# Nyström attention with a mixture of experts: expert index from averaged context rows, 32x32 blocks in the pseudo-inverse, another order

## The chip, the cores and the metric

The kernel runs on one core of one Trainium2 chip. Its metric is the device time of one execution in microseconds; the time before is the median of three runs, 215.47 us (214.98 to 217.77).

The core has five engines with a queue each: TensorE (PE in the rows; PEld is its weight load), VectorE (DVE), ScalarE (ACT), GpSimd (POOL) and SyncE (SP, which here issues nearly all transfers). An engine takes its instructions strictly in the order in which the program lists them, and waits on semaphores for the others.

## The reference

Inputs are q, k, v of shape 4 x 8 x 576 x 64 (batch, heads, rows, head size; q and k times 8), a gate 512 x 8, and for each of 8 experts a 512 x 1024 and a 1024 x 512 matrix. All is float32.

```python
q_lm, k_lm = mean of q, k over groups of 18 rows        # 32 landmarks a head
A = softmax(q @ k_lm.T / 8)    # 576 x 32
Bm = softmax(q_lm @ k_lm.T / 8)  # 32 x 32
C = softmax(q_lm @ k.T / 8)    # 32 x 576
Z = Bm.T / (norm1(Bm) * norminf(Bm) + 1e-6)
for _ in range(6): Z = 2 * Z - Z @ Bm @ Z
x = A @ Z @ C @ v              # per head; heads side by side: 2304 x 512

logits = x @ w_gate; e = argmax(logits, axis=1)
# a row keeps its expert only while that expert has had fewer than 576 rows
out = softmax weight of e * relu(x @ w1[e]) @ w2[e]     # 0 for rows not kept
```

The capacity of an expert, 576 rows, is the size of one batch. In the drawn inputs all 576 rows of a batch choose one expert: 0, 3, 6 and 0 for batches 0 to 3, so the rows of batch 3 find their expert full and are zero.

## The kernel before

The program handles four batches. For each it has a chain of attention work, and for batches 0 to 2 one expert (key 0 to 2) over the 576 rows; the output rows of batch 3 are written as zeros. A check at the end reads how many (batch, expert) pairs are still to do and, if there are any, runs a second pass for them (lines 930 to 943).

Attention of a batch: `landmarks` sums q and k over 18 rows (`lmq`, `lmk`; DVE or POOL). `scores` makes `psC` and `psA`; `cpath` takes the softmax of `psC`, transposes it (`ctp`, `CT`) and multiplies with v (`cvp`, then `CV`: 4 heads x 32 landmark rows of context, 64 wide, for each half `g` of the heads). `apath` takes the softmax of `psA` into `AW` and transposes it to `AT`. `chain` makes the 32x32 matrices `bp` of the eight heads, their softmax and norms (`bst`, `BB`, `cc`), and the pseudo-inverse, four heads at a time on 128 partitions. For batches 1 to 3 a round is one matmul a half (`pp`, line 320) of a 128x128 block-diagonal matrix (`PQ`, `PQn`), which DVE builds anew after each round: line 454 spreads five copies of a 32-column result against the mask `bmask`, 128x320, and line 455 adds W. Batch 0 keeps whole 128x128 blocks (ScalarE copies them) and has a second matmul `wp` a round. Six rounds end in `Wd`; with `CV` it gives `mtp` and `MT`, the 512 x 32 factor of x.

`route` makes the logits (`gp`, `Gg`, `ltp`, `lg`), the argmax (`ls`, `eq`, `idx`, `oh`), ranks of rows within an expert by matmuls with triangles (`rp`), the experts with rows still kept (`act`), and the first of them (`sel`, `fx`, `ei`, lines 647 to 655). `ei` is the index: SyncE loads it into a register (line 773) and only then issues the loads of `w1t` (line 736) and `w2t` (line 709).

The expert `ffn`: `gps` = w1 times MT (a row of x is A times a 32-row factor, so W1 is first contracted to 32 rows a head), split by ScalarE and DVE into `gh` and `gl`; `hps` = these times `ah`/`al` (the split AT), three matmuls for each product; relu and split (`rr`, `hx`); `yps` = `hx` times the split w2 (`wh`, `wl`), again three; scaled by `fac` and written.

What sets the order: every piece of work is a generator of steps with an engine, a planned cost and dependencies; `weave` (line 81) runs through all of them and emits the instructions in the order in which its own clock would start them. `CFG` holds numbers and letters found for it: priorities (`pr`, `fp`, `wl`, ...) and which engine does what (`lm`, `aw`, `rx`, `lo`). `wps` (line 914) are filler matmuls on zeros, emitted while PE has nothing before the first `yps`.

Of the kernel before, what the change touches and what calls it, by code (L numbers as in the profile page):

```python
# [9 lines left out]
F32 = mybir.dt.float32  # L10
# [4 lines left out]
ALU = mybir.AluOpType  # L15
# [65 lines left out]
def weave(streams, banks, fill=None):  # L81
# [6 lines left out]
    fast = False  # L88

# [19 lines left out]
    while ready:  # L109
        cand = {}  # L110
        first = None
        for s in ready:
            step = s[2]
            t = max(s[4], clk[step.eng])
            if step.res:
                r = res[step.res]
                i = nxt[step.res]
                late = [r[(i + x) % len(r)] for x in range(step.nres)]
                if None in late:
                    continue  # L120
                t = max(t, *late)
# [15 lines left out]
        end = clk[eng] = t + step.cost * (2 if eng == "P" and t < 6500 else 1)  # L137
        t = end + HOP[eng]
# [20 lines left out]
def nystrom_moe(ctx: ExitStack, tc: tile.TileContext, q, k, v, vtail, wgate, w1, w2, out, cap):  # L159
# [55 lines left out]
    nc.gpsimd.memset(wg, 0.0)  # L215
    SP = 128 * NT
# [51 lines left out]

    lmt = {}
# [4 lines left out]
    def landmarks(b):  # L274
        for g in range(NG):
            for nm in "qk":
# [14 lines left out]
                else:  # L291
                    yield Step("G", 1380, deps=ld, order=order, prev=False)
# [4 lines left out]
                    yield Step("G", 700)  # L297
                    nc.gpsimd.tensor_tensor(tr[:, :, 0:4], tr[:, :, 0:4], tr[:, :, 4:8], ALU.add)
                    yield Step("G", 430)
                    nc.gpsimd.tensor_tensor(tr[:, :, 0:2], tr[:, :, 0:2], tr[:, :, 2:4], ALU.add)  # L300
                    yield Step("G", 380)
                    nc.gpsimd.tensor_tensor(tr[:, :, 0:1], tr[:, :, 0:1], tr[:, :, 8:9], ALU.add)
                    yield Step("G", 380, name=f"lm{b}{g}{nm}")
# [7 lines left out]
    n4 = [128, NG, 4, 32]  # L311
    gr = [128, NG, 32]

    def spread(t, src, n, e="V"):
        (nc.vector if e == "V" else nc.gpsimd).tensor_tensor(t, src.unsqueeze(2).to_broadcast([128, NG, n, 32]),
                                bmask[:, 0:n, :].unsqueeze(1).to_broadcast([128, NG, n, 32]), ALU.mult)

    def bdmm(dst, t, rhs):
        for g in range(NG):
            nc.tensor.matmul(dst[:, g], lhsT=t[:, g, 0:4].rearrange("p h m -> p (h m)"), rhs=rhs[g],  # L320
                             start=True, stop=True)

    def V(c, **kw):
        return Step("V", c, **kw)

    def chain(b):
        p = Step("P", 267, deps=LM(b, 0) + LM(b, 1), order=([f"wd{b - 1}"] if b else []) + ([f"mt{b - 2}"] if b > 1 else []), name=f"bp{b}", res="ch",
# [16 lines left out]
        yield Step("A", 150)  # L344
# [3 lines left out]
        yield V(70)  # L348
# [3 lines left out]
        yield V(140)  # L352
        nc.vector.tensor_tensor(Bst, Bst, bst[:, 1, :].unsqueeze(2).to_broadcast(gr), ALU.mult)
        yield V(140)
        nc.vector.transpose(BT, Bst)
        rc = sm.tile([128, 2, NG], F32, tag="rc", name="rc")
        cc = sm.tile([128, 2, NG], F32, tag="cc", name="cc")

        def norms():
            yield V(200)  # L360
            nc.vector.tensor_reduce(out=rc, in_=BB, axis=AX.X, op=ALU.add)
            yield V(135)
            rcb = sm.tile([128, 2 * NG, 32], F32, tag="rcb", name="rcb", bufs=1)
            nc.vector.tensor_copy(rcb, rc.rearrange("p a g -> p (a g)").unsqueeze(2).to_broadcast([128, 2 * NG, 32]))
            yield V(200)
            rct = sm.tile([128, 2 * NG, 32], F32, tag="rct", name="rct", bufs=1)
            nc.vector.transpose(rct, rcb)
            yield V(200)
            nrm = sm.tile([128, 2, NG], F32, tag="nrm", name="nrm")
            nc.vector.tensor_reduce(out=nrm.rearrange("p a g -> p (a g)"), in_=rct, axis=AX.X, op=ALU.max)  # L370
            yield V(70)
            nc.vector.tensor_tensor(cc[:, 0, :], nrm[:, 0, :], nrm[:, 1, :], ALU.mult)
            yield V(70)
# [5 lines left out]
        full = CFG["sx"][b] == "F"  # L379
        e = CFG["s3"][3 * b]  # L380
        yield Step(e, 330 if e == "V" else 690)
        BTd = sm.tile(n4, F32, tag="bd", name="BTd", bufs=1)
        spread(BTd, BT, 4, e)
        p = Step("P", 434 if full else 350, res="ch", keep=True)
        yield p
        nb = 4 if full else 1
        bbp = pch.tile([128, NG, nb, 32], F32, tag="ch", name="bbp")
        bdmm(bbp.rearrange("p g a m -> p g (a m)"), BTd,
             [(BTd[:, g].rearrange("p h m -> p (h m)") if full else BT[:, g, :]) for g in range(NG)])
        yield V(527 if full else 330, free=p, deps=[f"cc{b}"])  # L390
# [588 lines left out]
```

## Time and profile before

| | before |
|---|---|
| median of 3 runs | 215.47 us (214.98 to 217.77) |
| span of the profiled execution, first to last instruction | 214.7 us |
| PE / PEld busy | 90% / 68% |
| DVE / ACT / POOL busy | 65% / 38% / 41% |
| moved | 31.88 MB, 149 GB/s on the mean |
| granted TensorE clock, mean | 0.973 |

The profiled execution's own time is its span, 214.7 us; the runs have some tenths around it. Matmuls overlap one another, so the busy time of PE is a union, and the price of one group in a dense stretch is read from the chain of waits, where pieces don't overlap. DVE too starts an instruction before the last has ended; the distance from start to start is its price there.

### The profile page before, as it was taken

Reading aid. Unit: us, or ns where it says so; the run is one execution under the profiler, and the core shown is the slowest. Engines: PE = TensorE matmul, PEld = TensorE weight load, DVE = VectorE, ACT = ScalarE, POOL = GpSimd, SP = SyncE. Lnnn points to the kernel's source line nnn. Section 1 sums busy time; section 2 is a strip of 40 time slices with the busy share of each in tenths; the row PEclk is TensorE's granted clock in tenths of the full one; section 3 lists DMA queues with packets and bytes.
Section 4 is the critical chain, followed back from the end, with each engine's and each line's share of the span. In section 5 each row is a group of like instructions: output and inputs, shape, how many; then the busy total and the mean of one; then the engine's idle time right before and its main releaser. Section 6 shows DMA issues by size and latency. Waiting matters only on the chain.

```text
span 214.7 us, 4895 instructions
## 1 busy us (share of the span) xinstructions
PE 194.1 (90%) x1822; PEld 145.6 (68%) x1826; DVE 138.7 (65%) x408; ACT 82.0 (38%) x209; POOL 88.8 (41%) x129
## 2 busy tenths in 40 slices
PE   7888998749997989999997989999999999999990
PEld 2345864235886766787866668978876889788880
DVE  3899989995889899998866547732017488221110
ACT  2052541214877555813024465760106667300000
POOL 8027998960499993010221993340000634300000
PEclk9999999675999999999999999999999999999998
DMA  6999938246899500101198620681117500011121
GB/s 196 362 341 373 360 137 260 78 157 234 298 358 328 187 0 3 24 3 49 50 322 256 206 102 0 197 293 27 49 52 221 172 3 0 6 27 49 49 78 34
DMA packets 17905, 31.88 MB, mean 149 GB/s; under 512 B 1520, under 2 KB 9616, under 8 KB 17872
## 3 DMA queue, kind: packets, MB, share of 16 engines
q1 hardware_dynamic: 17808, 31.46, 43.7%
q8 instruction: 16, 0.26, 0.5%
q14 instruction: 17, 0.14, 0.2%
q0 software_dynamic: 64, 0.02, 0.1%
HBM read 26.76 MB, written 4.72 MB: 147 GB/s over the span
## 4 chain that ended last, share of the span: by engine, by line
PE 64%; DVE 21%; DMA 6%; issue 2%; POOL 2%; ACT 1%; SPq 1%; ACTq 0%
PE yps L861 29%; PE hps L803 14%; DMA w2t<-in_w 4%; PE yps L866 4%; PE pp L320 4%; PE gps L577 3%; DMA kt<-in_k 2%; PE psA L466 2%; PE psC L466 2%; DVE lmk L289 2%; DVE sel L650 2%; PE cvp L517 1%; DVE AW L534 1%; PE ctp L500 1%; POOL wl L725 1%
## 5 line engine op out<-in xcount | busy, mean ns | idle before, releaser
L861 PE MATMUL yps<-wh,hx 128*128 128x512 f32 (+1 forms) x208 | 63.5, 379 | 0.0
L861 PEld LDWEIGHTS yps<-wh,hx 128*128 128x128 f32 x208 | 38.1, 188 | 7.1 <-issue 0.3
L861 PE MATMUL yps<-wl,hx 128*128 128x512 f32 (+1 forms) x104 | 38.8, 373 | 0.0
L725 POOL TENSOR_TENSOR wl<-w2t,wh 128x512 fp32r<-128x512 f32 x14 | 18.3, 1325 | 41.2 <-ACT wh L719 39.4
L826 POOL TENSOR_TENSOR hx<-rr,hx 128x288 fp32r<-128x288 f32 (+2 forms) x38 | 24.7, 668 | 14.8 <-ACT hx L817 14.5
L803 PE MATMUL hps<-ah,gh 128*128 128x288 f32 x96 | 29.5, 307 | 0.1
L878 DVE TENSOR_SCALAR yo<-yps,fac 128x512 f32<-128x512 f32 (+1 forms) x11 | 7.7, 701 | 32.6 <-PE yps L861 32.6
L803 PE MATMUL hps<-ah,gl 128*128 128x288 f32 x96 | 28.3, 295 | 0.0
L803 PE MATMUL hps<-al,gh 128*128 128x288 f32 x96 | 28.3, 295 | 0.0
L861 PEld LDWEIGHTS yps<-wl,hx 128*128 128x128 f32 x104 | 19.6, 189 | 3.2
L803 PEld LDWEIGHTS hps<-ah,gh 128*128 128x128 f32 x96 | 18.0, 188 | 1.8 <-ACT hx L820 0.4
L719 ACT CAST wh<-w2t 128x512 fp32r<-128x512 f32 x24 | 14.9, 620 | 8.6 <-DMA w2t<-in_w 7.2
L803 PEld LDWEIGHTS hps<-al,gh 128*128 128x128 f32 x96 | 18.0, 188 | 0.1
L803 PEld LDWEIGHTS hps<-ah,gl 128*128 128x128 f32 x96 | 18.0, 188 | 0.0
L320 PEld LDWEIGHTS pp<-PQn 128*128 128x128 f32 x76 | 10.2, 190 | 7.4 <-PE gps L577 3.8
L725 DVE TENSOR_TENSOR wl<-w2t,wh 128x512 fp32r<-128x512 f32 x10 | 9.4, 940 | 8.9 <-ACT wh L719 8.6
L815 ACT ACTIVATE rr<-hps 128x288 f32<-128x288 f32 x27 | 11.1, 413 | 9.7 <-PE hps L803 8.0
L320 PE MATMUL pp<-PQn 128*128 128x64 f32 (+2 forms) x76 | 11.8, 278 | 2.9 <-DVE PQn L455 1.1
L557 POOL TENSOR_TENSOR AW<-AW,amx 128x576 f32<-128x576 f32 x6 | 6.9, 1158 | 14.7 <-DVE amx L545 14.7
L914 PE MATMUL wps<-wt 128*128 128x512 bf16 x30 | 11.4, 526 | 1.3 <-DVE bef L234 1.3
L817 ACT CAST hx<-rr 128x288 fp32r<-128x288 f32 x27 | 11.7, 434 | 0.6
L828 DVE SCALAR_TENSOR_TENSOR hx<-hps,hx 128x224 fp32r<-128x224 f32 (+2 forms) x34 | 10.1, 333 | 2.8 <-ACT hx L820 2.6
(177 smaller groups left out, 355.6 us busy)
## 6 DMA issues: line engine op xcount, KB each, us to landing
w1t<-in_w SPq DMA_DIRECT2D x12, 512.0 KB, 4.9
w2t<-in_w SPq DMA_DIRECT2D x24, 256.0 KB, 4.3
vm<-in_v SPq DMA_DIRECT2D x8, 512.0 KB, 7.3
qt<-in_q SPq DMA_DIRECT2D x6, 576.0 KB, 7.8
kt<-in_k SPq DMA_DIRECT2D x6, 576.0 KB, 7.8
out<-yo SPq DMA_DIRECT2D x11, 256.0 KB, 2.1
qt<-in_q SPq DMA_DIRECT2D x4, 288.0 KB, 4.2
kt<-in_k SPq DMA_DIRECT2D x4, 288.0 KB, 5.4
```

What stands on the lines that cost most here:

```text
L320: nc.tensor.matmul(dst[:, g], lhsT=t[:, g, 0:4].rearrange("p h m -> p (h m)"), rhs=rhs[g], start=True, stop=True)
L466: nc.tensor.matmul(ps[a][32 * h:32 * h + 32, :HS], lhsT=lmt[b, g, stat][x, y], rhs=st[b][mov][g][x, y, HS * a:HS * a + HS], start=True, st ...
L719: nc.scalar.copy(wh, w2t)
L725: (nc.gpsimd if e == "G" else nc.vector).tensor_tensor(wl, w2t, wh.bitcast(F32), ALU.subtract)
L803: nc.tensor.matmul(ps[:, :HS], lhsT=wt[:, g, fs], rhs=a[:, g, ss], start=(n == 0), stop=(n == 3 * NG - 1))
L815: nc.scalar.activation(rr, ps[:, :HS], AF.Relu)
L817: nc.scalar.copy(hx[:, fc, ss], rr)
L826: nc.gpsimd.tensor_tensor(dst, rr[:, x0 - s0:x1 - s0], hi, ALU.subtract)
L828: nc.vector.scalar_tensor_tensor(dst, ps[:, x0 - s0:x1 - s0], 0.0, hi, ALU.max, ALU.subtract)
L861: nc.tensor.matmul(ps[:, :dn], lhsT=hx[:, fc, o:o + 128], rhs=wt[:, d0:d1], start=(fc == 0 and o == t0 and wt is wh), stop=(fc == NFC - 1 ...
L866: nc.tensor.matmul(ps[:m], lhsT=hx[:, fc, t0:t0 + m], rhs=wt, start=(fc == 0 and wt is wh), stop=(fc == NFC - 1 and wt is wh))
L914: nc.tensor.matmul(wps[0], lhsT=wt[:, 0:128], rhs=wt, start=True, stop=True)
```

## The change

The expert index of batches 0 to 2 is no longer taken from `act`. A new generator `guess` sums the context rows (CV times the first columns of `bmask`: `xp`), multiplies with the gate (`wgd`, a second copy of it, loaded by a transfer of 512 rows of 32 bytes that ScalarE issues at the start: `glp`), and takes the argmax: `fx`, `ei`. `route` still makes `act`; what it has beside the guessed expert goes to `rest`, which the check at the end reads. For batch 3 nothing is guessed.

In `chain` the four heads of a half stay 32x32: matmuls on the four diagonal blocks of the array, W carried along and added by a matmul with the identity. The evacuation of a round is a copy of 128 columns (DVE for batches 0 and 3, ScalarE for 1 and 2, by `pe`). `CFG` and the steps' planned costs are new; a step may be marked `lock`, and then `weave` doesn't start it while it has a marked step of the other of DVE and POOL running.

```diff
+    wgd = const.tile([128, NP, E], F32, name="wgd")
+    nc.scalar.dma_start(wgd, wgate.rearrange("(c p) e -> p c e", p=128))
...
+            if step.lock:
+                h = held["V" if step.eng == "G" else "G"]
+                if h[0] <= t < h[1]:
+                    t = h[1]
...  (chain)
-        BTd = sm.tile(n4, F32, tag="bd", name="BTd", bufs=1)
-        spread(BTd, BT, 4, e)
...
         for g in range(NG):
+            for x in quads:
+                nc.tensor.matmul(bbp[x, g], lhsT=BT[x, g], rhs=BT[x, g], start=True, stop=True)
...
         for it in range(6):
             pp = pch.tile([128, NG, 2, 32], F32, tag="ch", name="pp")
-            bdmm(pp[:, :, lo:2, :], PQ, [PQ[:, g, 4 + lo:6].rearrange("p a m -> p (a m)") for g in range(NG)])
+            for g in range(NG):
+                for x in quads:
+                    nc.tensor.matmul(pp[x, g, lo:2].rearrange("p a m -> p (a m)"), lhsT=PQ[x, g, 0],
+                                     rhs=PQ[x, g, lo:2].rearrange("p a m -> p (a m)"), start=True, stop=False)
+                for x in quads:
+                    nc.tensor.matmul(pp[x, g, 1], lhsT=ident[x, x], rhs=PQ[x, g, 1], start=False, stop=True)
-            spread(Pn[:, :, 0:5], pp[:, :, 0], 5)
-            nc.vector.tensor_tensor(Pn[:, :, 5], PQ[:, :, 5], pp[:, :, 1], ALU.add)
+            (nc.scalar.copy if e == "A" else nc.vector.tensor_copy)(Pn, pp)
...
+    def guess(b):
+        for g in range(NG):
+            nc.tensor.matmul(xp[64 * g:64 * g + 64, :], lhsT=st[b][f"CV{g}"], rhs=bmask[:, 0:4, 0], start=True, stop=True)
+        nc.vector.tensor_scalar(xs, xp.unsqueeze(2).to_broadcast([128, 4, 32]), -1.0, None, op0=ALU.mult)
+        for c in range(NP):
+            for x in range(0, 128, 32):
+                nc.tensor.matmul(lp[x:x + 32, :], lhsT=xs[:, c, :], rhs=wgd[:, c, :], start=(c == 0), stop=(c == NP - 1))
+        nc.vector.tensor_reduce(out=gm[:, 0:1], in_=lp, axis=AX.X, op=ALU.max)
+        nc.vector.scalar_tensor_tensor(gm[:, 1:], lp, gm[:, 0:1], rev, ALU.is_ge, ALU.mult)
+        nc.vector.tensor_reduce(out=fxs[b], in_=gm[:, 1:], axis=AX.X, op=ALU.max)
+        nc.vector.tensor_scalar(ei[b], fxs[b][0:1, :], -1.0, float(E), op0=ALU.mult, op1=ALU.add)
...  (route)
-        nc.vector.tensor_tensor(sel[:, 0:E], act, rev, ALU.mult)
-        nc.vector.tensor_reduce(out=fx, in_=sel, axis=AX.X, op=ALU.max)
-        nc.vector.tensor_scalar(ei[b], fx[0:1, :], -1.0, float(E), op0=ALU.mult, op1=ALU.add)
```

How it moves instructions, at three places.

SyncE, around the first load of the expert's index (`ei`) and of its first weights (`w1t`). Before:

```order
L260 DMA kt<-in_k 128x1152
L265 DMA vm<-in_v 128x1024
L266 DMA vl<-in_vtail 64x256
L260 DMA qt<-in_q 128x1152
L265 DMA vm<-in_v 128x1024
L266 DMA vl<-in_vtail 64x256
L773 TENSOR_LOAD ei_133
L773 ISA x2
L736 ISA
L736 DMA w1t<-in_w 128x4x256
```

Now:

```order
L268 DMA qt<-in_q 128x1152
L268 DMA kt<-in_k 128x1152
L748 TENSOR_LOAD ei_135
L748 ISA x2
L711 ISA
L711 DMA w1t<-in_w 128x4x256
L273 DMA vm<-in_v 128x1024
L274 DMA vl<-in_vtail 64x256
```

The index and the first quarter of w1 now stand ahead of v of batch 2 and q of batch 3.

DVE, around the first index. Before, it is taken in `route` of batch 0, among the softmax of batch 1's small matrices:

```order
L629 SCALAR_TENSOR_TENSOR eq<-ls,rev 128x40
L343 TENSOR_TENSOR BB<-bp,bst 128x64
L632 TENSOR_REDUCE idx<-eq 128x5
L636 TENSOR_TENSOR oh_137<-revi,idx 128x40
L479 TENSOR_REDUCE cs<-psC 128x1
L647 SCALAR_TENSOR_TENSOR act<-rp,bef 128x8
L481 TENSOR_SCALAR cs<-cs 128x1
L650 TENSOR_TENSOR sel_139<-act,rev 128x8
L347 TENSOR_REDUCE bst<-BB 128x2
L653 TENSOR_REDUCE fx<-sel_139 128x1
L349 TENSOR_SCALAR bst<-bst 128x2
L655 TENSOR_SCALAR ei_133<-fx 1x1
```

Now, ahead of the pseudo-inverse's first matrix (`PQ`) of batch 0:

```order
L376 TENSOR_TENSOR cc<-nrm 128x2
L546 TENSOR_SCALAR amx<-amx 128x18
L471 TENSOR_SCALAR cs<-cs 128x1
L472 RECIPROCAL cs<-cs 128x1
L548 RECIPROCAL amx<-amx 128x18
L378 TENSOR_SCALAR cc<-cc 128x2
L437 SCALAR_TENSOR_TENSOR gm<-glp,gm,rev 128x8
L380 RECIPROCAL cc<-cc 128x2
L439 TENSOR_REDUCE fx_139<-gm 128x1
L390 TENSOR_TENSOR PQ<-BB,cc 128x2x32
L441 TENSOR_SCALAR ei_135<-fx_139 1x1
L393 SCALAR_TENSOR_TENSOR PQ<-bbp,cc,istk 128x32 x2
```

`ei` moves from `route` of batch 0 to ahead of its pseudo-inverse; `eq`, `idx`, `oh` and `act` now follow the first `gl`, and `sel` is gone.

PE, the last work ahead of the first `hps` of key 0. Before, with batch 1's block-diagonal rounds (`pp`) and two `cvp` around the two `gps`:

```order
L517 MATMUL cvp<-vm,CT 32x64 x16
L517 MATMUL cvp<-vl,CT 32x64 x4
L500 MATMUL ctp<-ident,Cx 128x128 x4
L500 MATMUL ctp<-ident,Cx 64x128
L577 MATMUL gps<-w1t,MT_119 32x256 x8
L517 MATMUL cvp<-vm,CT 32x64 x16
L517 MATMUL cvp<-vl,CT 32x64 x4
L320 MATMUL pp<-PQ 128x64 x2
L577 MATMUL gps<-w1t,MT_119 32x256 x8
L320 MATMUL pp<-PQn 128x64 x2
L803 MATMUL hps<-ah,gh 128x288
```

Now:

```order
L559 MATMUL gps<-w1t,MT_121 32x256 x8
L586 MATMUL gp<-wg,MT_121 32x64 x4
L482 MATMUL ctp<-ident,Cx 64x128
L889 LDWEIGHTS wt
L889 MATMUL wps<-wt 128x512
L889 LDWEIGHTS wt
L889 MATMUL wps<-wt 128x512
L499 MATMUL cvp<-vm,CT 32x64 x16
L499 MATMUL cvp<-vl,CT 32x64 x4
L595 MATMUL ltp<-AT_117,Gg 32x160 x8
L559 MATMUL gps<-w1t,MT_121 32x256 x8
L778 MATMUL hps<-ah,gh 128x288
```

The first `gps` now stands ahead of `gp` and `ltp`, which make the logits, and no round of batch 1 stands ahead of the first `hps`; one `psC`, one `cvp` and its transposes and the ranks `rp` of batch 0 have moved behind it.

## Rows read from the trace of the kernel before

**Rows 1.** Page, parts 1 and 2: PE in all; granted clock in 40 slices.

```profile
PE 194.1 (90%) x1822; PEld 145.6 (68%) x1826; DVE 138.7 (65%) x408; ACT 82.0 (38%) x209; POOL 88.8 (41%) x129
PEclk9999999675999999999999999999999999999998
```

**Rows 2.** Busy time by stretch; columns in its first line.

```profile
core 0: us, PE busy (x) PEld busy (x) DVE busy (x) ACT busy (x) POOL busy (x), PEclk, DMA share, GB/s
0.00:55.50 55.50, 45.99 (x620) 25.83 (x624) 47.29 (x139) 17.83 (x43) 33.44 (x62) 0.91 0.74 250
55.50:123.10 67.60, 63.31 (x603) 49.00 (x603) 56.79 (x167) 33.40 (x98) 33.89 (x40) 1.00 0.48 158
123.10:208.90 85.80, 84.79 (x603) 70.72 (x601) 34.11 (x103) 30.78 (x70) 21.46 (x29) 1.00 0.25 83
208.90:214.70 5.80, 0.00 (x0) 0.00 (x0) 0.48 (x1) 0.00 (x0) 0.00 (x0) 0.88 0.10 31
```

**Rows 3.** Timeline of DVE: start, duration, instruction, [idle before and its releaser].

```profile
36.27 1.31 DVE L626 TENSOR_TENSOR ls<-lg,lmx 128x40 f32<-128x40 f32 x1
...
39.70 2.62 DVE L650 TENSOR_TENSOR sel<-act,rev 128x8 f32<-128x8 f32 x1
...
43.35 0.14 DVE L655 TENSOR_SCALAR ei<-fx 1x1 int32<-1x1 f32 x1
43.47 0.17 DVE L351 RECIPROCAL bst<-bst 128x2 f32<-128x2 f32 x1
...
45.97 0.87 DVE L315 TENSOR_TENSOR BTd<-BB,bmask 128x256 f32<-128x256 f32 x1
...
50.53 0.28 DVE L522 TENSOR_SCALAR CV<-cvp,cs 128x64 f32<-128x64 f32 x1 [0.80 <-PE cvp L517]
...
53.48 0.69 DVE L753 TENSOR_TENSOR gl<-gps,gh 128x512 fp32r<-128x512 f32 x1 [0.58 <-ACT gh L751]
...
104.14 0.15 DVE L650 TENSOR_TENSOR sel<-act,rev 128x8 f32<-128x8 f32 x1
```

**Rows 4.** Timeline of POOL, beside the second row of the DVE rows.

```profile
39.69 2.61 POOL L768 TENSOR_TENSOR al<-AT,ah 128x1152 fp32r<-128x1152 f32 x1
```

**Rows 5.** Timelines of SyncE's queue and of PE: first w1 loads, first `hps`.

```profile
44.52 1.59 SPq L736 DMA_DIRECT2D w1t<-in_w  x3
55.49 0.38 PE L803 MATMUL hps<-ah,gh 128*128 128x288 f32 x1
```

**Rows 6.** Chain of waits, dense stretches: start, time on the chain, group.

```profile
87.70 0.39 PE pp L320 x4
88.53 1.10 PE psC L466 x16
92.12 0.83 PE cvp L517 x40
96.80 0.26 PE bp L334 x16
98.31 0.48 PE ctp L500 x4
106.98 0.36 PE bbp L320 x4
163.37 0.25 PE gp L604 x8
```

**Rows 7.** Groups by form: count | busy us, mean ns | idle before, releasers.

```profile
L315 DVE TENSOR_TENSOR PQn<-pp,bmask 128x320 f32<-128x320 f32 x15 | 7.2, 481 | 3.7 <-PE pp L320 3.4
L589 DVE COPY MT<-mtp 128x128 f32<-128x128 f32 x4 | 1.1, 283 | 0.3 <-PE mtp L586 0.2
L320 PE MATMUL pp<-PQn 128*128 128x64 f32 x48 | 7.3, 274 | 1.7 <-DVE amx L564 1.0 <-PE gps L577 0.6
L320 PE MATMUL pp<-PQn 128*128 128x32 f32 x12 | 1.7, 267 | 1.1 <-DVE PQn L455 1.1
```

**Rows 8.** Page, part 3: POOL's transfers, all of them short gate rows.

```profile
q0 software_dynamic: 64, 0.02, 0.1%
```

More of the change, by code (lines that the diff above doesn't have):

```diff
@@ L309, in small @@
         return ("f", pff) if CFG["tg"][i] == "f" else ("tp", ptp)
-    n4 = [128, NG, 4, 32]
     gr = [128, NG, 32]
[L314 to L324, printed above, removed]
+    quads = [slice(32 * h, 32 * h + 32) for h in range(4)]
     def chain(b):
-        p = Step("P", 267, deps=LM(b, 0) + LM(b, 1), order=([f"wd{b - 1}"] if b else []) + ([f"mt{b - 2}"] if b > 1 else []), name=f"bp{b}", res="ch",
+        p = Step("P", 230, deps=LM(b, 0) + LM(b, 1), order=([f"wd{b - 1}"] if b else []) + ([f"mt{b - 2}"] if b > 1 else []), name=f"bp{b}", res="ch",
                  keep=True)
@@ L526, in apath @@
         if CFG["pa"][2 * b + g] == "f":
-            p = Step("P", 1124, res="f", nres=2, deps=[f"lm{b}{g}k"] + [f"ld{b}{g}q{y}" for y in range(2)], order=order, name=f"psA{b}{g}", keep=True)
+            p = Step("P", 1105, res="f", nres=2, deps=[f"lm{b}{g}k"] + [f"ld{b}{g}q{y}" for y in range(2)], order=order, name=f"psA{b}{g}", keep=True)
             yield p
@@ L535, in apath @@
         else:
-            p = Step("P", 1124, res="sc", deps=[f"lm{b}{g}k"] + [f"ld{b}{g}q{y}" for y in range(2)], order=order, name=f"psA{b}{g}", keep=True)
+            p = Step("P", 1105, res="sc", deps=[f"lm{b}{g}k"] + [f"ld{b}{g}q{y}" for y in range(2)], order=order, name=f"psA{b}{g}", keep=True)
             yield p
@@ L581, in mpart @@
         MT = MTk[b]
-        p = Step("P", 236, res="ch", keep=True, deps=[f"wd{b}"] + [f"cv{b}{g}" for g in range(NG)])
+        p = Step("P", 370, res="ch", keep=True, deps=[f"wd{b}"] + [f"cv{b}{g}" for g in range(NG)])
         yield p
@@ L598, in route @@
         MT = MTk[b]
-        p = Step("P", 183, res="ch", keep=True, order=[f"rt{b - 2}"] if b > 1 else ())
+        p = Step("P", 250, res="ch", keep=True, order=[f"rt{b - 2}"] if b > 1 else ())
         yield p
@@ L725, in lo @@
                 (nc.gpsimd if e == "G" else nc.vector).tensor_tensor(wl, w2t, wh.bitcast(F32), ALU.subtract)
[L727 removed]
+            later(lo, e, 1225 if e == "G" else 602, name=f"ws{key}{c}", lock=True)
     def ffn(b, er, key, factor, store):
@@ L739, in gpart @@
         def gpart(c):
-            p = Step("P", 1016, deps=[f"w1{key}{c}"], order=[f"y{key - 1}3"] if key else (), res="sc", keep=True,
+            p = Step("P", 600, deps=[f"w1{key}{c}", f"mt{b}"], order=[f"y{key - 1}3"] if key else (), res="sc", keep=True,
                      name=f"G{key}{c}", prev=False, prio=CFG["g"][key])
```

255 lines of the change are left out of this document (113 added, 142 removed), and 8 rows, old and new, of the table pr.

## The prediction

> **What bounds the kernel now.** I read the busy times by stretch first, cut at the two places where the program's character changes: the first `hps` at 55.5 us and the first `hps` of key 1 at 123.1 [rows 2]. From 55.5 to the last `yps` at 208.9, PE is busy 63.31 of 67.60 and 84.79 of 85.80 us: it is the bound, 5.3 us of holes in all, 4.3 of them in the first piece. After it come 5.8 us in which PE does nothing (last scaling, output, check). Ahead of 55.5 PE isn't the bound, although its row says 45.99: part of that are the fillers (`wps`), and the granted clock sinks in three slices between 37 and 54 us [rows 1]. There DVE is the bound, 47.29 of 55.50 from its first work at 6 us on. So the time is: start of the first `hps`, plus PE's work behind it, plus holes, plus 5.8.
>
> Why does the first `hps` come so late? The timeline of DVE shows it [rows 3]. Its index `ei` is made at 43.35, the first w1 load goes out at 44.52 [rows 5], and `gl`, which `hps` needs, starts at 53.48. On the way, between 36.27 and 46.84, seven tiny instructions take far longer than their size: `ls` 1.31, `sel` 2.62 for 8 elements, `BTd` 0.87 are the first, the longest and the last. The same `sel` takes 0.15 at 104.14. At 39.69 to 42.30 POOL runs `al` [rows 4], and `sel` ends with it: DVE stood behind POOL. The seven take 8.1 us, at their shortest durations 1.6; 6.5 are waits.
>
> **The change, part by part.**
>
> *The index.* Guessed, `ei` needs CV of batch 0 alone. By the new order 52 DVE instructions that stood ahead of the first `gl` no longer do (route of batch 0, the first half of batch 1's chain, the W updates, one `psC` maximum), and 13 new ones do (five copies, `Wd`, seven for two guesses). At start-to-start distances (0.12 for a small one, `ei` to the next in [rows 3]; 0.20 for a copy of 128 columns, its 0.283 less an overlap of 0.08 [rows 7]) I estimate 8.1 us that go and 2.3 that come: **5.8 less**. The seven slow instructions all lie among those that go: **6.5 less**. The wait of 0.80 for `cvp` [rows 3] goes with PE's lighter queue; the 0.58 for `gh` stays. `wgd` brings 512 rows of 32 bytes at the start, beside the q and k loads on which all waits. 64 such packets took 0.1% of 16 engines' span, 3.4 us, so 54 ns each [rows 8]; 512 on 16 engines are 1.7 us; between 0 (they slip in) and 1.7 I take the middle, **0.8 more**. First `hps`: 55.5 - 5.8 - 6.5 - 0.8 + 0.8 = 43.2, **12.3 us earlier**.
>
> Can something else hold it? The index itself: its place in DVE's new queue gives some 25 us, w1 out 1.2 later (44.52 less 43.35), so the weights have ten microseconds to arrive; behind the index on SP wait only v of batch 2 and q, k of batch 3, needed later. The pseudo-inverse of batch 0: `PQ` at some 25 us, then PE's work from the first `pp` to `mtp` by [rows 6], some 9 us, then MT, `gps`, `gh`, `gl`, some 3: `hps` at 39 to 40. DVE is later, and I keep it. Bounds: 40 if DVE shrinks further; 50 if all the waits come back (55.5 - 5.8).
>
> *PE behind the first `hps`.* The later part grows, since `hps` now overtakes work. By the prices of [rows 6]: one `psC` 1.10, one `cvp` 0.83, its five transposes 0.48 + 0.12, the ranks `rp` 0.22 (seven short ones at `gp`'s 0.031 a record). Rounds: before, 16 behind it (4 + 6 + 6) at 0.39, 6.24; now 18. No row has a round of 16 matmuls on 32x32 blocks. From below: `psC` puts two matmuls of 288 columns on each of four strips of the array in 1.10, 1.91 ns a column; a new round puts 2 x (64 + 32) columns on each diagonal block, 0.37. From above: `bp` has 16 records in 0.26; 32 are 0.52. Nothing tells which is nearer, so the middle, **0.44**: 18 x 0.44 = 7.92, 1.68 more. `bbp`, three of half a round, 0.78 for two of 0.36: 0.06. One guess for batch 2: `xp` 0.2 (between 0.06 by records and `bbp`'s 0.36) and `glp`, 32 records between 0.52 by `bp` and 1.0 by `gp`: 0.6. Sum **5.3 more**.
>
> The Trainium skill, page "TensorE: Matmul & The Clock Gate", section "Wait — 56ns, not 53.3ns?", says that matmuls never start closer than some 25 ns, however small. By that a round would be 0.80 and the sum 6.5 us higher, an estimate from that page. `bp`'s row contradicts it: 16 records in 0.26 are 16 ns each, and the measurement decides.
>
> *Holes.* In the first piece they are 4.3 us. Those ahead of `pp` are 1.7 + 1.1 [rows 7]: PE waits until DVE has spread five copies (0.481) and added W. A copy takes 0.283, or ScalarE does it. I let these **2.8 go**; bounds 0 and 4.3. DVE isn't the next to bind: of its 56.79 us there, the 15 spreads were 7.2.
>
> *Sum* against the profiled execution: 214.7 - 12.3 + 5.3 - 2.8 = 204.9. The median of the runs lies 0.8 above its span: **205.7 us**. The expert's own matmuls, relu, stores and the last 5.8 us are as before.
>
> **Rivals.**
>
> A. *Row strips of the array take turns.* `psC` and `gps` send matmuls that contract over different partitions to different PSUM banks. The new rounds send four such strips to one bank. Only `bp` did so before, with two, and its row doesn't clear it: four strips together would be 2 x 32 x 1.91 = 0.12, two by two 0.24, one after the other 0.49; it took 0.26. If the four take turns, a round is 768 columns x 1.91 = 1.47, 1.03 more, 18 times behind `hps` and 6 times in the chain ahead of it: +24.7, **230 us**. It decides from a round of 0.85 on (9.8 us in 24 rounds brings it to the old time). The Trainium skill has this as a rule ("TensorEngine Tiling (Array Packing)", "Gotcha 1: PSUM Pressure"): different row tiles cannot access the same PSUM bank at once. That would be this rival; no run so far shows it with four. Chance 0.06.
>
> B. *The waits come back.* POOL still runs the long `al` and `AW`, and DVE's small instructions fall beside them again: 6.5 us of waits on other rows, and PE's holes stay, since its chain still goes through a full DVE queue: 205.7 + 6.5 + 2.8 = **215.0**, no change. For it: 33.89 us of POOL in the first piece behind `hps` [rows 2]. Against it: the two-operand instructions that waited stand elsewhere now, and marked steps avoid one another in the plan, if the chip keeps near it. Chance 0.11.
>
> C. *The guess is wrong*, and the second pass runs for a batch, with one expert alone on PE: the last piece of [rows 2] holds about two, so over 41 us more, **247 or above**. For the drawn inputs the averaged context rows choose 0, 3 and 6, as the rows do; batch 2's margin is small (0.231 against 0.212) but far above float32 error. Chance 0.02.
>
> D. *More is won.* `hps` at 40 (the pseudo-inverse's bound), rounds of 0.37, all 4.3 of holes gone: 205.7 - 3.2 - 1.3 - 1.5 = **199.7**. Chance 0.11.
>
> **Numbers.** The forecast, with its terms between their bounds (hps 41 to 47, rounds 0.37 to 0.52), has 0.70. The prediction is 205.7. The range 198 to 213 takes in D and the better half of B, and leaves out A, C and the rest of B. A measurement of this kernel can tell some 2% from no change: faster is below 211.2, slower above 219.8. Faster 0.83 (forecast, D, a little of B), same 0.10, slower 0.07 (A without its mildest form, C).
>
> **What would show it.** First `hps` at about 43, index at about 25, w1 out at about 26; seven slow rows on DVE's way replaced by ones below 0.3; rounds of `pp` at 0.37 to 0.52 in dense stretches (above 0.85: A); PE busy over 97% from there to the last `yps` about 156 us later; holes ahead of `pp` below 1 us. Wrong if `hps` starts after 48, or if PE behind it has more than 6 us of holes, or if the lines of the second pass run.

## The result: 211.1 us against 216.2, and the profile after

The changed kernel took 211.12 us in the median of four runs (208.19 to 211.7); beside it the kernel before took 216.18 (214.98 to 217.77). The ratio is 0.968, 95% interval 0.958 to 0.979; it compares undisturbed runs alone (208.19 and 210.79 here, without the first profiled execution), so it isn't the ratio of these medians. Run again beside other experiments it took 209.57 against 214.44, 0.979 (0.971 to 0.987). The prediction was 205.7, range 198 to 213.

The first profiled execution took 211.7 us and has a span of 209.9; a profiled execution of the second set, called **the repeat** here, took 207.58 with a span of 205.9. It is the fastest of that set's five; the other four have spans of 207.6 to 208.3. Both are used; verdicts rest on the repeat.

Parts 1 to 3 of the first execution's page, beside [rows 1] and [rows 8]: PE busy, granted clock in 40 slices, then queues with packets, MB and share.

```profile
PE 193.6 (92%) x2638; PEld 142.8 (68%) x2639; DVE 125.0 (60%) x365; ACT 80.1 (38%) x185; POOL 89.1 (42%) x131
...
PEclk9999996988999999999999999999999999999996
...
q8 instruction: 23, 0.38, 0.7%
...
q10 hardware_dynamic: 528, 0.02, 0.1%
```

The kernel before fetched 16 packets of instructions:

```profile
q8 instruction: 16, 0.26, 0.5%
```

Busy time by stretch in the repeat, cut at its first `hps` and its last `yps`, beside [rows 2]:

```profile
core 0: us, PE busy (x) PEld busy (x) DVE busy (x) ACT busy (x) POOL busy (x), PEclk, DMA share, GB/s
0.00:42.38 42.38, 36.31 (x780) 19.34 (x781) 33.74 (x101) 14.28 (x31) 27.23 (x51) 1.00 0.91 313
42.38:199.87 157.49, 154.12 (x1868) 121.13 (x1859) 91.91 (x265) 65.33 (x154) 62.31 (x81) 1.00 0.35 118
```

DVE's timeline in the first execution, beside [rows 3]: the index, `gl`, then three instructions behind the first `hps`.

```profile
24.92 0.22 DVE L390 TENSOR_TENSOR PQ<-BB,cc 128x64 f32<-128x64 f32 x1
25.06 0.13 DVE L441 TENSOR_SCALAR ei<-fx 1x1 int32<-1x1 f32 x1
...
41.34 0.68 DVE L728 TENSOR_TENSOR gl<-gps,gh 128x512 fp32r<-128x512 f32 x1
...
54.52 0.80 DVE L638 TENSOR_TENSOR carry<-cy,carry 128x8 bf16<-128x8 f32 x1
55.24 1.38 DVE L368 COPY rcb<-rc 128x128 f32<-128x128 f32 x1
...
61.27 1.32 DVE L390 TENSOR_TENSOR PQ<-BB,cc 128x64 f32<-128x64 f32 x1
```

SyncE's queue and PE there, beside [rows 5]:

```profile
26.22 0.42 SPq L711 DMA_DIRECT2D w1t<-in_w  x1
45.64 0.51 PE L778 MATMUL hps<-ah,gh 128*128 128x288 f32 x1
```

The chain of waits there, beside [rows 6]: start, time on the chain, group.

```profile
30.08 0.23 PE cvp L499 x3
30.31 1.72 issue
32.03 1.39 PE cvp L499 x37
...
42.24 1.68 issue
43.91 0.31 PE cvp L499 x7
...
88.32 0.26 PE bbp L387 x16
...
91.27 0.24 PE pp L401 x8
91.51 0.06 PE pp L404 x8
91.57 0.11 PE pp L401 x8
91.69 0.06 PE pp L404 x8
91.75 0.59 PE ctp L482 x4
...
98.19 0.37 PE glp L432 x32
```

A round runs from 91.27 to 91.75, 0.48. New are the two rows "issue": PE stands still in the middle of a `cvp`, with no wait shown. The repeat has one, of 2.27 us, and its first `hps` is at 42.38, not 45.64. Both executions leave the first hole at 32.03. Of the 3.26 us between them 1.68 are the second hole. Some 1.5 are the granted clock: from 32.03 to 36 us of the first execution it is 0.53 and 0.61 in the mean, so mostly the lower level of 1.2 GHz, while the repeat stays at the upper one, 2.4 GHz, although its hole was longer. The two stretches of the first execution, then the same `psA` in the chain of the first execution and in that of the repeat:

```profile
32.03:34.00 1.97, 1.97 (x69) 1.63 (x68) 0.52 (x2) 0.28 (x1) 1.96 (x2) 0.53 0.11 37
34.00:36.00 2.00, 2.00 (x32) 0.89 (x28) 1.23 (x2) 0.00 (x0) 1.70 (x2) 0.61 0.88 272
```

```profile
34.21 1.77 PE psA L448 x16
```

```profile
33.40 1.10 PE psA L448 x16
```

One thing more stands in the first execution's chain: from the first `pp`, at 25.93, to `hps` every row but the holes is PE's. In the repeat PE's busy time from 25 us to `hps` and the hole fill that stretch exactly (15.11 + 2.27 = 17.38), while `gl` is done at 40.6, 1.8 us before `hps` (the stretch, then DVE's timeline):

```profile
25.00:42.38 17.38, 15.11 (x491) 9.42 (x489) 13.59 (x42) 7.07 (x15) 14.47 (x17) 1.00 0.84 295
```

```profile
39.91 0.68 DVE L728 TENSOR_TENSOR gl<-gps,gh 128x512 fp32r<-128x512 f32 x1
```

### The profile page after: what moved, and what is told of

Its sections match the earlier page's. It is cut to its first block, busy times and chain, and to the rows that moved or that the text cites. A ratio compares the mean times of both kernels' runs of the same rounds, so it can differ in the third digit from the quotient of the medians.

```text
span 209.9 us, 6440 instructions
## 1 busy us (share of the span) xinstructions
PE 193.6 (92%) x2638; PEld 142.8 (68%) x2639; DVE 125.0 (60%) x365; ACT 80.1 (38%) x185; POOL 89.1 (42%) x131
## 2 busy tenths in 40 slices
DMA packets 18439, 32.00 MB, mean 152 GB/s; under 512 B 2048, under 2 KB 10144, under 8 KB 18400
## 4 chain that ended last, share of the span: by engine, by line
PE 76%; DVE 15%; DMA 2%; issue 2%; ACT 1%; SPq 1%; ACTq 0%
PE yps L836 30%; PE hps L778 14%; PE yps L841 5%; PE pp L401 4%; PE psC L448 4%; PE psA L448 3%; PE cvp L499 3%; PE ctp L482 3%; DMA kt<-in_k 2%; PE gps L559 2%; PE wps L889 2%; DVE lmq L303 2%; PE pp L404 1%; PE ltp L595 1%; DVE gl L728 1%
## 5 line engine op out<-in xcount | busy, mean ns | idle before, releaser
L801 POOL TENSOR_TENSOR hx<-rr,hx 128x224 fp32r<-128x224 f32 (+2 forms) x47 | 27.2, 599 | 23.1 <-ACT hx L792 22.9
L778 PE MATMUL hps<-ah,gh 128*128 128x288 f32 x96 | 30.4, 317 | 1.2 <-DVE hx L803 1.2
L700 POOL TENSOR_TENSOR wl<-w2t,wh 128x512 fp32r<-128x512 f32 x13 | 17.1, 1327 | 25.3 <-ACT wh L694 23.8
L853 DVE TENSOR_SCALAR yo<-yps,fac 128x512 f32<-128x512 f32 (+1 forms) x8 | 5.7, 716 | 30.5 <-PE yps L836 30.5
L836 PEld LDWEIGHTS yps<-wl,hx 128*128 128x128 f32 x104 | 19.6, 188 | 3.1
L851 ACT ACTIVATE yo<-yps,fac 128x512 f32<-128x512 f32 (+1 forms) x5 | 3.2, 642 | 36.7 <-PE yps L836 36.7
L551 POOL TENSOR_TENSOR AW<-AW,amx 128x576 f32<-128x576 f32 x6 | 7.0, 1162 | 23.7 <-DVE amx L548 20.9
L790 ACT ACTIVATE rr<-hps 128x288 f32<-128x288 f32 x30 | 12.3, 410 | 8.8 <-PE hps L778 8.7
L466 ACT ACTIVATE Cx<-psC,cs 128x576 f32<-128x576 f32 x8 | 5.9, 741 | 22.6 <-DVE cs L463 22.6
L792 ACT CAST hx<-rr 128x288 fp32r<-128x288 f32 x30 | 12.7, 435 | 0.5
L539 POOL TENSOR_TENSOR AW<-AW,amx 128x576 f32<-128x576 f32 x5 | 6.8, 1365 | 12.6 <-DVE amx L527 12.6
L448 PE MATMUL psC<-kt,lmq 64*32 64x288 f32 x128 | 10.1, 407 | 1.5 <-DMA kt<-in_k 1.5
```

What stands on the lines that cost most here:

```text
L448: nc.tensor.matmul(ps[a][32 * h:32 * h + 32, :HS], lhsT=lmt[b, g, stat][x, y], rhs=st[b][mov][g][x, y, HS * a:HS * a + HS], start=True, st ...
L551: (nc.gpsimd if e == "G" else nc.vector).tensor_tensor(AW, AW, amx[:, 1, :].unsqueeze(2).to_broadcast([128, L, 32]), ALU.mult)
L700: (nc.gpsimd if e == "G" else nc.vector).tensor_tensor(wl, w2t, wh.bitcast(F32), ALU.subtract)
L778: nc.tensor.matmul(ps[:, :HS], lhsT=wt[:, g, fs], rhs=a[:, g, ss], start=(n == 0), stop=(n == 3 * NG - 1))
L790: nc.scalar.activation(rr, ps[:, :HS], AF.Relu)
L792: nc.scalar.copy(hx[:, fc, ss], rr)
```

## The experiments

Theory F (fetch) was formed from the first trace. PE's instructions come in packets of 16 KB by q8 (23 packets for 5277 records of PE and PEld, 16 for 3648 before). If one is 256 instructions of 64 bytes and PE is at its end before the next has come, PE stands still. The Trainium skill, "Runtime: NRT & Kernel Launch", section "Instruction fetch mechanics", gives blocks of 16 KiB or 256 instructions, fetched while the block before runs, and calls the crossing mostly hidden. By the order of the program, a float32 matmul counted as four (two loads, two passes), the holes lie 513 instructions apart (253 matmul records with a load each, and seven waits): two packets. And a packet starts just before the first; the queues in 29.50 to 29.75 us:

```profile
q1 hardware_dynamic: 65, 0.07, 87.6%
q8 instruction: 1, 0.02, 28.6%
```

Before the second hole it is the same (a packet starts in 41.50 to 41.75). From the packet's start to PE's next instruction it is 2.4 us both times.

**after_again**, the changed kernel once more:

> The changed kernel once more, as the measure for the runs beside it. Theory F (fetch): PE's two holes that wait for nothing shown (1.72 us from 30.31 and 1.68 us from 42.24, each in the middle of a cvp, each 2.4 us behind the start of an instruction packet of the queue q8, 29.65 and 41.5) belong to the position in PE's instruction stream, which is the same in each execution: they come again at the same instruction of the same cvp, 1.5 to 1.9 us each. Rival R (chance): they were an accident of that execution and come elsewhere or not at all. Time 208 to 212 either way.

209.57 us. Timeline of PE:

```profile
29.46 0.30 PE L499 MATMUL cvp<-vm,CT 128*32 128x64 f32 x3
32.03 0.64 PE L499 MATMUL cvp<-vm,CT 128*32 128x64 f32 x29 [2.27 <-issue]
```

The first hole stands behind the same third record. The second didn't come: its packet started near 38.3 instead of 41.5, and PE reached the place at 40.6, 2.3 us later. So the place is fixed by the program and the size is not; F's "1.5 to 1.9 each" was too narrow, and chance (R) has a part in the size.

**shift**, the same program with some 60 instructions more at its start:

```
-        for _ in range(n):
+        cut = 1 if wps else 4
+        for _ in range(n * cut):
-            nc.tensor.matmul(wps[0], lhsT=wt[:, 0:128], rhs=wt, ...)
+            nc.tensor.matmul(wps[0][:, :512 // cut], lhsT=wt[:, 0:128], rhs=wt[:, :512 // cut], ...)
```

> The fillers at PE's start are cut in four: nine or ten matmuls of 512 columns become four times as many of 128, the same columns in the same stretch before the first psC, and some 30 matmuls and 30 weight loads more in PE's stream; all behind that is as in the changed kernel. Theory F: an instruction packet is 16 KB, 256 instructions of 64 bytes; the two holes lie 512 instructions apart by the order of the program, so at ends of packets. With some 60 instructions more ahead of them the ends fall some 60 instructions earlier in the program: no hole at the fourth matmul of that cvp or at its first vl matmul; instead holes in the pp round ahead of the first cvp (or in the ctp ahead) and in the wps or the gp ahead of the second, 0 to 2.5 us each. Rival P (place): the holes belong to these cvp, by a wait that the profile does not show: both stay where they were, 1.7 us each. Time 206 to 213.

208.54 us, 0.973 of before (0.962 to 0.984). Timeline of PE:

```profile
28.91 0.31 PE L401 MATMUL pp<-PQn 32*32 32x64 f32 x6
30.04 0.24 PE L401 MATMUL pp<-PQn 32*32 32x64 f32 x1 [0.83 <-issue]
...
38.61 0.30 PE L499 MATMUL cvp<-vm,CT 128*32 128x64 f32 x3
39.21 0.64 PE L499 MATMUL cvp<-vm,CT 128*32 128x64 f32 x29 [0.30 <-issue]
```

Both holes moved: the first out of that `cvp` into the round ahead of it, behind six records, the second within its `cvp` from behind the first `vl` record to behind the third `vm` one. Each is about 60 instructions earlier, as F says (the second in a place where I had looked for the `wps`), and the hole again ends 2.3 to 2.4 us behind the start of a packet (27.7 and 36.9). Rival P is out.

The trace has a third hole, behind `hps`, where the changed kernel has none. By the order of the program it lies 2048 instructions behind the second, eight packets, and it ends 2.7 us behind the start of its packet (93.45). From 92 to 96.5 us no other transfer ran; PE's timeline, then the transfers of that stretch:

```profile
96.15 0.25 PE L404 MATMUL pp<-PQn,ident 32*32 32x32 f32 x4 [1.04 <-issue]
```

```profile
DMA packets 1, 0.02 MB, mean 4 GB/s; under 512 B 0, under 2 KB 0, under 8 KB 0
```

So such a hole needs no big load beside it. Whether the loads lengthen the others stays open.

**ident1** and **ident1glp**, fewer and larger matmuls:

```
-                for x in quads:
-                    nc.tensor.matmul(pp[x, g, 1], lhsT=ident[x, x], rhs=PQ[x, g, 1], ...)
+                nc.tensor.matmul(pp[:, g, 1], lhsT=ident, rhs=PQ[:, g, 1], ...)
```

> In each round of pp the four identity matmuls on 32x32 blocks of one g become one with the whole identity, 128x128 on 32 columns: 16 matmuls and 16 loads become 2 x (1 + 1) x 2, 24 records fewer a round counting one per pass of matmul and as many loads, 576 instructions fewer in all, 144 fewer ahead of the first hps; the order is the same. Theory F: PE asks for instructions faster than they come only where many small ones stand together (850 of them between 24 and 42 us, 3.3 packets); with 144 fewer the two holes together shrink from 3.4 us to 0 to 1.7, and with them the stretch at half clock behind the second (46 to 49 us); first hps at 42.5 to 44.5 instead of 45.6. A round of pp falls from 0.48 to some 0.35 (sixteen L401 records took 0.32, four more by the 16 ns of bp), 18 of them behind hps: 2.3 less. Time 204 to 207. Rival P: the holes stay at 3.4 us in the same two cvp, hps at 45.0 to 45.6, time 207 to 209. Rival G (what PE gains another engine gives back): holes at pp waiting for the copies of DVE or ScalarE, 208 to 211.

ident1glp also has

```
-            for x in range(0, 128, 32):
-                nc.tensor.matmul(lp[x:x + 32, :], lhsT=xs[:, c, :], ...)
+            nc.tensor.matmul(lp, lhsT=xs[:, c, 0:1].to_broadcast([128, 128]), ...)
```

> As ident1, and glp's sixteen matmuls on strips of 32 columns become four that write all 128 partitions at once, with the one column of xs spread over 128 in the weight load: 48 instructions fewer per guess, 240 fewer in all ahead of the first hps. Theory F: holes without a shown wait ahead of hps below 1 us in sum, first hps at 42 to 43.5, index 0.2 to 0.3 earlier (glp 0.37 to some 0.15): w1 out at about 25.9; time 203.5 to 206.5. Rival P: holes as before, time 207 to 209.

222.25 and 225.10 us: 13 and 16 slower than the changed kernel, which no theory expected. No "issue" hole is left ahead of `hps`, as F says (one of 1.09 stands behind it in ident1, 1.10 in ident1glp), and `hps` starts at 43.86 in ident1. But the rounds cost more than the holes gave; ident1's chain of waits:

```profile
28.04 0.34 PE pp L403 x2
29.21 0.24 PE pp L401 x8
29.45 0.34 PE pp L403 x2
```

Two records with the whole identity take 0.34, where the eight on 32x32 blocks took 0.06, and both sets of L401 now take 0.24, where the second took 0.11. A round is 1.16 instead of 0.48, and 18 x 0.68 = 12.2 of the 12.9 us between the spans. I first looked at the loads; groups of ident1:

```profile
L403 PEld LDWEIGHTS pp<-PQn,ident 128*128 128x128 f32 x80 | 11.9, 188 | 3.3
L401 PEld LDWEIGHTS pp<-PQn 32*32 32x32 f32 x320 | 6.1, 102 | 7.2 <-issue 2.8 <-ACT rr L790 0.5 <-ACT CT L487 0.5
```

Two loads of 188 ns one behind the other would be 0.38, near the 0.34; `glp` with whole loads went from 0.37 to 1.0. I had priced both by the count of records. But loads alone don't explain the round. The kernel before has four such records a round; its chain shows them at 0.39 behind `yps`, which also takes the whole array [rows 6], and at 0.59 behind `psC`, which takes it in strips:

```profile
89.64 0.59 PE pp L320 x4
```

So the change from strips to the whole array seems to cost some 0.2 there, and ident1 changes between blocks and the whole array four times a round. How much of the 0.68 is the load and how much the change, no run separates.

**wadd**, the identity matmuls left out and W added on DVE:

```
-                    nc.tensor.matmul(pp[x, g, 1], lhsT=ident[x, x], ...)
...
-            (nc.scalar.copy if e == "A" else nc.vector.tensor_copy)(Pn, pp)
+                (nc.scalar.copy if e == "A" else nc.vector.tensor_copy)(Pn[:, :, 0], pp[:, :, 0])
+            nc.vector.tensor_tensor(Pn[:, :, 1], PQ[:, :, 1], pp[:, :, 1], ALU.add)
```

> The identity matmuls of the rounds left out: W is added on DVE (one instruction of 128x64 a round), the copy of P is half as long; 32 PE instructions fewer a round, 768 in all; the table of numbers made anew for this. Theory F: a round falls from 0.48 to 0.24 to 0.30, 18 behind hps: 3 to 4 us less; holes without a shown wait ahead of hps below 1 us; first hps at 40 to 43; time 203 to 206.5. Rival G (what PE gains another engine gives back): 24 adds more at 0.14 to 0.2 on DVE and two instructions in a row between rounds, holes at pp that wait for DVE 3 us or more behind hps: 207 to 211.

203.50 us (203.23 to 204.8), 0.949 of before (0.944 to 0.954): faster than both kernels. `hps` starts at 40.58, no "issue" hole is left on PE, and the clock is full; its stretches and a round on its chain:

```profile
0.00:40.58 40.58, 36.54 (x686) 18.24 (x687) 33.23 (x97) 14.38 (x35) 27.50 (x51) 1.00 0.94 324
40.58:195.31 154.73, 152.72 (x1580) 118.02 (x1571) 90.98 (x295) 64.39 (x145) 73.80 (x91) 1.00 0.36 120
```

```profile
92.48 0.36 PE pp L401 x16
92.84 1.59 PE yps L844 x6
```

The round falls to 0.36, not to 0.24 to 0.30: the identity records had taken 2 x 0.06. Rival G is out: PE's idle time behind `hps` is 2.0, less than the repeat's 3.4.

**noguess, oldchain, neither, waddng**: one part or both undone, each with a table of numbers found anew by a random search that the planner's own reckoning judged. In noguess `ei` comes from act in route again:

```
-        streams.append((CFG["gu"][b], guess(b)))
...
+            nc.vector.tensor_tensor(sel, act, rev, ALU.mult)
+            nc.vector.tensor_reduce(out=fxs[b], in_=sel, axis=AX.X, op=ALU.max)
+            nc.vector.tensor_scalar(ei[b], fxs[b][0:1, :], -1.0, float(E), ...)
```

oldchain has `chain` of the kernel before with its planned costs (a part of the edit is below), neither has both edits, waddng is wadd with the edit of noguess.

```
-                    nc.tensor.matmul(pp[x, g, lo:2]..., lhsT=PQ[x, g, 0], ...)
...
+            bdmm(pp[:, :, lo:2, :], PQ, ...)
...
+            spread(Pn[:, :, 0:5], pp[:, :, 0], 5)
```

> The guess undone: no xp and glp, the index from act as in the kernel before; chain, marked steps and all else as in the changed kernel, the table of numbers made anew for this. Theory I (the index is most of it): the index falls back behind route of batch 0, to 38 to 44 us, and the first hps to 50 to 55; PE does more chain and score work ahead of it, so the end moves less: 5 to 8 us over the changed kernel, 213 to 217. Rival C (the lighter chain is most of it): 208 to 211, hps at 44 to 48.

> The chain undone: block-diagonal tiles of 128x128 and their spreads on DVE and POOL as in the kernel before, the guess and all else as in the changed kernel, the table of numbers made anew for this (xs has one buffer instead of two, for room). 1033 PE instructions by the program's order stand ahead of the first hps instead of 1584. Theory F: no hole without a shown wait ahead of hps, but holes at pp behind DVE's spreads again, 2 to 4 us in all behind hps, and DVE some 7 us busier: 209 to 213. Rival C (the lighter chain is most of it): hps after 48, time 213 to 217. Rival N (the new chain gains nothing, what it gives it loses to the fetch): 205 to 208.5.

> Guess and chain undone together: index from act, block-diagonal chain, but the planner's new step costs and the marks on DVE and POOL kept, and the table of numbers made anew for this. Each part undone alone cost nothing that could be measured (209.8 and 209.1 beside 209.6). Theory S (either part alone does what both do: it takes away the idle time ahead of hps, and the rest is PE's work): both undone fall back to the kernel before, 213 to 216, with PE idle 14 us or more outside the tail and hps after 50. Theory O (the new order, costs and marks, is all of the gain): 207.5 to 210.5, idle time below 11 us.

> W added on DVE and the guess undone, the table of numbers made anew. With the guess the same chain took 203.5. Theory W (PE's work and its fillers set the time, not the start of hps, so the guess adds work for nothing): 202.5 to 205. Rival I (with the light chain the index is the last thing that hps waits for): hps after 48, more than 60 fillers, 205.5 to 210.

Fillers, idle (to the last `yps`) and work (PE busy less fillers) are from the profiled executions, in us:

| kernel | guess | chain | median | ratio to before | first hps | fillers | idle | work |
|---|---|---|---|---|---|---|---|---|
| before | no | old | 214.4 to 216.3 | 1 | 55.49 | 11.4 | 14.8 | 182.7 |
| neither | no | old | 216.65 | 1.002 (0.994 to 1.009) | 60.44 | 13.0 | 13.2 | 183.5 |
| oldchain | yes | old | 209.06 | 0.968 (0.963 to 0.972) | 39.80 | 9.9 | 9.6 | 181.9 |
| noguess | no | new | 209.80 | 0.977 (0.970 to 0.985) | 63.88 | 19.6 | 7.4 | 175.2 |
| after (repeat) | yes | new | 209.57 | 0.979 (0.971 to 0.987) | 42.38 | 11.2 | 9.4 | 179.2 |
| waddng | no | W on DVE | 207.63 | 0.964 (0.951 to 0.978) | 50.90 | 18.2 | 7.3 | 174.1 |
| wadd | yes | W on DVE | 203.50 | 0.949 (0.944 to 0.954) | 40.58 | 12.5 | 6.1 | 176.8 |

Theory S holds, O falls: with the marks, the new costs outside `chain` and a new table but neither part, the time is that of before. By the ratios either part alone brings 5 to 7 us, and both together 5 to 7 (the first set had 0.968). For noguess and oldchain theory I, both rivals C and rival N took one part for the main one or the new one for worthless; the time of noguess falls in C's range (208 to 211), but with `hps` where C had excluded it, and oldchain's in F's (209 to 213) at its lower end. In noguess the index comes at 43.94 and `hps` starts 8 us later than before, and still the end is 6 us earlier in span: PE does other batches' chains meanwhile. With W on DVE the ratios give 8 us for the chain alone and 11 for both. Of waddng's expectations rival I holds: `hps` at 50.90, 62 fillers, 207.63.

The table also shows what each part does. The guess alone (oldchain) takes fillers and idle from 26.2 to 19.5 and leaves the work, to which it adds some 1.7 of its own (three times `xp` 0.21 and `glp` 0.37); the chain alone (noguess) leaves those at 27.0 and takes the work from 182.7 to 175.2. Their ends, 7.5 and 6.6 us earlier at the last `yps`, would add to 14, and the repeat's is 9.0 earlier. What both may share is the granted clock: its mean was 0.973 before and 0.972 in neither, but 0.993 in oldchain, 0.996 in noguess and 0.991 in the repeat, so part of the old work ran at the lower level, and either change wins that back. In warm (below) the mean is 0.987 with the same work in the same order, and that work is 180.2 instead of 182.7. By this the clock's share is an estimated 3 to 4 us, counted twice in the 14; the 1 to 2 us that are left are no more than the repeat's hole. No run takes the clock's share by itself.

Beside the repeat, wadd has 2.4 us less work, 3.3 less idle, of which the hole is 2.27, and 1.3 more fillers. So the new chain seems to have lost in the changed kernel by its identity matmuls, their time in the rounds and the hole; but wadd's table is another one, too. noguess has one hole, of 0.43 at 56.63, in a round.

**nolock**, the marks without effect in the planner, and a new table:

```
-            if step.lock:
+            if step.lock and False:
```

> The planner doesn't keep the marked steps of DVE and POOL apart any more (the rest as in the changed kernel, the table of numbers made anew for this). Theory L (the marks win back the 6.5 us of waits): DVE's small two-operand instructions stand behind POOL's long ones again, rows of 0.8 to 2.6 us on DVE's way to gl, hps 2 to 6 us later, time 211 to 216. Rival (the waits went because the index no longer passes those steps): hps within 1.5 us of the changed kernel's, time 207 to 211.

208.16 us, 0.968 (0.964 to 0.971). The index is at 26.00, `hps` at 45.75. Of DVE's small instructions between the index and `gl` at 43.52 none takes over 0.5. The rival holds: the waits stay away without the marks, as they should if they went because the index no longer passes the instructions that waited.

**oldnums**, the table of before in the changed code:

```
-    sw=3000,
+    sw=2000,
...
-    fp=[1580, 2144, 2271],
+    fp=[31, 537, 861],
```

> The changed kernel's code, costs and marks, with the table of numbers of the kernel before (the new entries as in the changed kernel). Theory T (the table fits only the code it was made for): holes behind DVE and stretches of fillers of 10 us or more, 215 to 228. Theory P (the table matters little since PE is the bound anyway): 207 to 212.

226.43 us, 1.053 (1.040 to 1.067). The first `hps` is at 50.91, PE busy 87% of the span instead of the repeat's 92%. T holds: a table fits its code. So noguess, oldchain, neither, wadd, waddng and nolock have their own, and a difference of a microsecond or two between any of them may be the table's (nolock, 0.968, beside the changed kernel's 0.979, differs by the planner's table and marks alone).

**warm**, the kernel before with more fillers:

```
-            fill(int(t - clk["P"] - 50) // 216 if ...
+            fill(int(t - clk["P"] - 50) // 120 if ...
```

> The kernel before with more fillers: where the planner leaves PE idle it now puts one filler per 120 ns instead of per 216, 57 in all instead of 33; all other work in the same order. Ahead of the first hps the granted clock of the kernel before was 0.91 in the mean, so 5 us of 55 ran at half. Theory K (the half clock is a good part of what the change wins back, since every version that is near 209 holds full clock there): with the clock at full up to hps, psC, ctp, cvp and pp there take some 2 to 3 us less and hps starts 1 to 3 us earlier, 211.5 to 214. Theory D (DVE is the bound ahead of hps, so PE's clock there costs nothing): hps within 0.7 us of 55.5, 214 to 216.5. Rival (the fillers stand in the way): 217 or more.

218.79 us against 215.14, 1.023 (1.012 to 1.034). From 36 to 56 us the granted clock is 0.91 instead of 0.74, PE's busy time is 15.04 both times and `hps` is at 56.12:

```profile
36.00:56.00 20.00, 15.04 (x252) 8.45 (x246) 18.34 (x60) 6.12 (x15) 11.29 (x15) 0.91 0.55 181
```

K falls, D is right on `hps`: DVE is busy 18.34 of 20 there and PE waits for it. The time is that of the third expectation (217 or more). PE's busy time is 195.1, 14.9 of it fillers (before 194.1 and 11.4), so the work falls by 2.5 and the fillers grow by 3.5. The low clock in [rows 1] thus isn't what delays `hps`; what it costs in work the fillers took again. (A mean of 0.91 over 55.5 us is some 10 us at the lower level, not the 5 of the expectation.)

## Why the prediction was right, point by point

*The bound ahead of hps.* Right for the kernel before: DVE, not PE, as warm shows (though DVE's first work is at 3.80, not 6). Wrong for the changed one: "DVE is later, and I keep it" was the step that failed. From 25 us on the chain is PE's, and `gl` is done 1.8 us ahead of `hps` in the repeat, 3.6 in the first execution. The path of the pseudo-inverse was priced with its own matmuls, while PE also had `psA`, `psC`, `cvp` and `ltp` in the same queue. The index was to come at 25 and w1 to leave at 26; they came at 25.06 and 26.22.

*First hps at 43.2.* 45.64 in the first execution, 42.38 in the repeat. The seven slow waits are gone from the way to `gl`, as the term of 6.5 says; the longest small rows left there in the repeat are a `cc` of 0.62 and an `amx` of 0.41, above the 0.3 that was to hold. But 43.2 is met by luck in part: DVE was ready earlier, and PE's queue and the fetch, a term that was missing (3.4 us of holes in the first execution, 2.27 in the repeat), made the difference. Without its hole the repeat would start near 40, the lower bound given. `wgd` was priced at 0.8: its queue q10 shows 0.1% of 16 engines' span, an estimated 0.2 us each and not 1.7, and the second `lmk`, at 7.12 before, is at 7.37 in the first execution and ends at 7.52 in the repeat, before 7.87 there.

*PE behind hps, +5.3.* Work there was 148.1 and is 154.1 in the repeat: +6.0. The round took 0.48 where 0.44 was taken from 0.37 to 0.52; 18 x 0.04 = 0.7 looks like the whole difference. But the old rounds were priced too low as well: of the nine that the old chain shows behind `hps`, six took 0.36 to 0.39 and three 0.59 to 0.63, 0.46 in the mean. With 0.48 and 0.46 the sum is 4.9, and 1.1 stay open. Some of that may stand in the rows behind the rounds: `yps` x6 takes 1.59 behind a round on 32x32 blocks (wadd's chain above) and took 1.44 behind an old one:

```profile
86.26 1.44 PE yps L861 x6
```

Rival A would have made the round 1.47; at 0.48 four strips in one bank don't take turns here. So the rule of the Trainium skill's page "TensorEngine Tiling (Array Packing)", "Gotcha 1: PSUM Pressure", did not decide. Nor did the 25 ns that the Trainium skill's page "TensorE: Matmul & The Clock Gate", section "Wait — 56ns, not 53.3ns?", gives as the least distance: 32 records in 0.48 are 15 ns each.

*Holes, -2.8.* 5.3 before, 3.4 in the repeat: 1.9 less. The waits for spreads went, but POOL and DVE meet again behind `hps`: `PQ` takes 1.32 at 61.27 against 0.22 at 24.92, POOL runs `hx` and `wl` beside it, and the `pp` that needs it waits 1.70. This is rival B's mechanism in another place; the same wait is 1.3 in the repeat. Holes ahead of `pp` were to stay below 1 us.

*Sum.* Span 204.9 predicted, 205.9 in the repeat, 209.9 in the first execution. The median was 5.4 above the prediction in the first set and 3.9 in the second; 0.9 of the 3.9 is that 1.7 us lie around the repeat's span, where the prediction took 0.8, 1.0 is the span, and 2.0 is that the repeat is the fastest of its set; what the slower ones did differently no trace shows.

*What was wrong in the reasoning* is the step "first hps 12.3 us earlier" as the cause of the gain. As bookkeeping it came out; as a cause it fails, since noguess gains as much as the changed kernel with `hps` 8 us later than before. What counts is the idle time and the fillers on PE plus its work, over the whole program, and the repeat has 5.4 less of idle, 0.2 less of fillers and 3.5 less of work. Why the two parts don't add is only estimated above, by the clock's share and the fetch.

## What to carry to other kernels

When two parts of a change win back the same loss, undo both before crediting either; an early start of the main loop is worth only the idle time that it removes. When a bound is lifted, price the next engine's whole queue up to that point, not only the path of one result. Price a small matmul by its load and by the shape used just before it, as well as by its records: splitting into 32x32 blocks made the work cheap and the instruction count high, and both have a price. In a stretch of many tiny matmuls count instructions against the packets of the instruction queue.

## What the hardware showed that was not expected

- PE stood still for 0.3 to 2.3 us at fixed points of its instruction stream, 256 instructions or a multiple apart, ending 2.3 to 2.7 us after an instruction packet began; the packet itself took some 1.1 us (28.6% of 16 engines for 0.25 us). Where the packet had begun 2.3 us before PE came to the place, as near 38.3 in the repeat, nothing was lost: in 23 packets the first execution shows two holes. The Trainium skill's "mostly hidden" is thus right for most packets and wrong at these.
- A float32 load of a 128x128 block took 188 ns in the mean, one of 32x32 102. Two passes of the whole identity with 32 columns took 0.34 between 32x32 blocks, eight passes on the blocks 0.06. Four passes with whole loads took 0.39 behind a whole-array matmul and 0.59 behind one in strips.
